# One pool of seven PSUM banks, and ScalarE's measured pace in the planner of a fused attention and MLP kernel

## The chip, the cores and the metric

The kernel runs on one core of a Trainium2 chip. The metric is the time of one execution on the device in microseconds (us); the span in a profile runs from the first to the last instruction and is about 1.8 us shorter. PE is TensorE, ACT is ScalarE, DVE is VectorE, POOL is GpSimd, SP is SyncE.

## The reference

```python
def reference(A_x, A_wq, A_wk, A_wv, A_wo, B_x, B_w1, B_w2):
    # x: 2048 x 512 bf16; 32 query heads of 16, one key head and one value head
    xn = layernorm(x)
    q = (xn @ wq) split into 32 heads; k = xn @ wk; v = xn @ wv
    s = softmax(q k^T / 4) v, heads joined, @ wo
    h = silu(xn @ w1)             # 512 -> 1792
    g = silu(h @ w2)              # 1792 -> 512
    return x + s * g
```

Scores are 32 heads x 2048 queries x 2048 keys. The exponentials of this many numbers are the bulk of the work outside TensorE. (The code of the reference, which is longer, is put here in short form.)

## The kernel before

The program is not written down instruction by instruction. A planner simulates the five engines with assumed durations and latencies, picks the next instruction for each engine, and emits what it picked; on the chip, semaphores enforce the dependencies, and each engine keeps the planned order.

A score tile is 128 keys x 512 queries of one head, f32, one PSUM bank. There are 2048 of them. A tile goes one of two ways. ScalarE takes two or three banks in one `Exp` instruction and writes bf16, which then needs one value product on PE. Or VectorE converts the tile to an integer whose bits are an approximate exponential; GpSimd (or VectorE) makes three shifted copies, and the tile then needs four value products.

```python
A_BANKS = ((0, 1, 2), (3, 4, 5))      # two halves for ScalarE
OB = 6                                # accumulates the value products of a group
POOL_BANKS = (7,)                     # everything else: projections, VectorE's tiles
...
LAT = {                               # ns from an instruction's end to its being seen
    (PE, AC): 221.0, (PE, DV): 221.0, (PE, PE): 0.0,
    (AC, PE): 402.0, (AC, DV): 390.0, (AC, AC): 250.0, ...
...
def s_phase_ready():                  # may PE start the next score phase?
    ub = st["fill"] % 2
    banks = A_BANKS[ub]
    if len(units) >= 2 and units[-2].exp is None:
        return None
    if lent.get(ub) is not None and lent[ub].op is None:
        return None
    ...
    for b in banks:                   # all three banks of the half
        r = max(r, pl.ready(PE, (), [("ps", b)]))
...
op = pl.place(AC, 0.8333 * NQ * n + T_AF, lambda a: a.activation(
    pa_sb[:, s * NQ:(s + n) * NQ], ps[:, b0 * 512:(b0 + n) * 512], ACT.Exp), ...)
```

Score matmuls use four row tiles of 32 and fill up to four banks at once. Value products, projections and the MLP use four column tiles of 32; I call four such matmuls a round. In the listings below, L756 (before) and L776 (after) are the score matmuls, L1056 and L1079 the value products, L458 and L466 the projections and the MLP, L1297 and L1341 the exponentials, L937 and L962 VectorE's score conversions.

The softmax here doesn't subtract the row's maximum and nothing guards it: scores larger than these inputs give would overflow.

## Time and profile before

| | before |
|---|---|
| time, median | 716.7 us |
| span of the profiled run | 715.0 us |
| ScalarE busy | 676.6 us, 95% |
| tiles on ScalarE / on VectorE | 1392 / 656 |
| exp instructions (3, 2, 1 banks) | 93, 556, 1 |

One warning ahead: the mean length of a record is not an engine's pace, since ScalarE's records overlap.

### The profile page before, as it was taken

The numbers are of one execution on the slowest core, as the hardware profiler recorded it, in microseconds if no ns is written. First come the engines' busy times: TensorE is split into PE (matmuls) and PEld (weight loads), VectorE is DVE, ScalarE is ACT, GpSimd is POOL, SyncE is SP. The second block draws the span as 40 slices with busy tenths as digits, with TensorE's granted clock in tenths as the row PEclk, the third lists the DMA queues.
The fourth block names the chain that finished last, engine by engine and source line by source line (L and its number), as shares of the span: only waits on it lengthen the run. The fifth ranks groups of instructions, "written<-read, shape, count | busy, mean of one in ns | idle before, by whom it ended". The sixth has DMA issues, their size and how long they took to land.

```text
span 715.0 us, 20429 instructions
## 1 busy us (share of the span) xinstructions
PE 669.9 (94%) x8693; PEld 191.2 (27%) x8693; DVE 604.8 (85%) x1039; ACT 676.6 (95%) x729; POOL 484.6 (68%) x472
## 2 busy tenths in 40 slices
PE   5799999999999999999999999998999999999996
PEld 3332222222222222222222222222232222222233
DVE  8778889989889898888887898899888898899865
ACT  3699999999999999999999999999989999999992
POOL 2037777877866777867777768778626677878780
PEclk9899999999999999999999999999999999999999
DMA  9300000000000000000000000000000000000000
GB/s 314 101 17 1 2 2 2 2 1 3 2 2 2 23 25 17 2 1 2 2 2 2 1 3 24 24 17 1 2 2 2 2 1 17 17 17 17 2 2 31
DMA packets 11434, 12.61 MB, mean 18 GB/s; under 512 B 1809, under 2 KB 10769, under 8 KB 11345
## 3 DMA queue, kind: packets, MB, share of 16 engines
q1 hardware_dynamic: 10288, 11.28, 4.9%
q8 instruction: 70, 1.15, 0.7%
q10 hardware_dynamic: 1056, 0.03, 0.1%
q14 instruction: 20, 0.16, 0.1%
HBM read 8.95 MB, written 2.10 MB: 15 GB/s over the span
## 4 chain that ended last, share of the span: by engine, by line
ACT 79%; PE 12%; DVE 7%; issue 1%; DVEq 0%
ACT pa_sb L1297 75%; PE ps L1056 4%; ACT t_sb L584 4%; PE ps L458 4%; PE ps L756 3%; DVE db_sb L937 2%; DVE ds_sb L991 1%; DVE stats_sb L405 1%; ACT t_sb L607 1%; PE ps L474 1%; DVE f_sb L1073 0%; DVE otr_sb L1077 0%; DVE xn_sb L434 0%; PE ps L500 0%; DVE fin_sb L621 0%
## 5 line engine op out<-in xcount | busy, mean ns | idle before, releaser
L1297 ACT ACTIVATE pa_sb<-ps 128x1024 bf16<-128x1024 f32 (+1 forms) x650 | 660.8, 1282 | 13.7 <-PE ps L756 12.0
L996 POOL INT64_ADD ds_sb<-db_sb x461 | 480.7, 1059 | 212.4 <-PE ps L1056 143.9
L937 DVE TENSOR_SCALAR db_sb<-ps 128x512 uint16<-128x512 f32 x656 | 436.4, 685 | 68.7 <-PE ps L756 62.3
L756 PE MATMUL ps<-qt_sb,kt_sb 32*128 32x512 bf16 x2048 | 256.1, 385 | 21.7 <-ACT pa_sb L1297 10.4
L1056 PE MATMUL ps<-ds_sb,v_sb 128*32 128x512 bf16 x1968 | 228.1, 383 | 0.9 <-DVE ds_sb L991 0.5
L1056 PE MATMUL ps<-pa_sb,v_sb 128*32 128x512 bf16 x1392 | 215.6, 384 | 0.3 <-ACT pa_sb L1297 0.3
L1056 PE MATMUL ps<-db_sb,v_sb 128*32 128x512 bf16 x656 | 154.4, 384 | 6.4 <-DVE f_sb L1073 6.3
L756 PEld LDWEIGHTS ps<-qt_sb,kt_sb 32*128 32x128 bf16 x2048 | 65.8, 91 | 305.9 <-ACT pa_sb L1297 245.7
L1056 PEld LDWEIGHTS ps<-ds_sb,v_sb 128*32 128x32 bf16 x1968 | 56.8, 95 | 55.7 <-issue 36.9
L458 PE MATMUL ps<-xnT_sb,w_sb 128*32 128x512 bf16 x896 | 69.2, 384 | 0.3 <-DVE db_sb L937 0.3
L458 PE MATMUL ps<-w_sb,u_sb 128*32 128x512 bf16 x896 | 68.5, 384 | 0.9 <-DVE db_sb L937 0.9
L1056 PEld LDWEIGHTS ps<-pa_sb,v_sb 128*32 128x32 bf16 x1392 | 54.8, 95 | 36.5 <-issue 23.3
L1056 PEld LDWEIGHTS ps<-db_sb,v_sb 128*32 128x32 bf16 x656 | 38.2, 95 | 29.8 <-DVE f_sb L1073 12.8
L584 ACT ACTIVATE t_sb<-ps 128x512 bf16<-128x512 f32 x56 | 46.0, 822 | 0.0
L586 DVE SCALAR_TENSOR_TENSOR u_sb<-t_sb,ps 128x512 bf16<-128x512 bf16 x56 | 38.1, 681 | 9.1 <-ACT t_sb L584 8.2
L991 DVE TENSOR_SCALAR ds_sb<-db_sb 128x2048 uint16<-128x2048 uint16 x31 | 26.5, 871 | 1.8 <-PE ps L1056 1.6
L458 PEld LDWEIGHTS ps<-w_sb,u_sb 128*32 128x32 bf16 x896 | 17.0, 94 | 29.3 <-issue 22.4
L1073 DVE STREAM_TRANSPOSE f_sb<-ps 128x512 f32<-128x512 f32 x32 | 22.7, 708 | 1.5 <-PE ps L1056 1.2
L458 PEld LDWEIGHTS ps<-xnT_sb,w_sb 128*32 128x32 bf16 x896 | 14.8, 94 | 27.5 <-issue 21.5
L609 DVE SCALAR_TENSOR_TENSOR tmp_sb<-t_sb,ps 128x512 bf16<-128x512 bf16 x16 | 11.0, 685 | 11.4 <-ACT t_sb L607 11.3
L458 PE MATMUL ps<-xnT_sb,wq_sb 128*32 128x512 bf16 x256 | 20.0, 399 | 0.0
L1077 DVE TENSOR_TENSOR otr_sb<-f_sb,rcp_sb 128x256 bf16<-128x256 f32 x32 | 18.7, 588 | 0.2
(54 smaller groups left out, 168.9 us busy)
## 6 DMA issues: line engine op xcount, KB each, us to landing
w_sb<-in_B_w_dram SPq DMA_DIRECT2D x2, 1792.0 KB, 13.0
xr_sb<-in_A_x_dram SPq DMA_DIRECT2D x16, 128.0 KB, 2.6
out_dram<-ob_sb SPq DMA_DIRECT2D x16, 128.0 KB, 1.7
ds_sb<-in_A_x_dram SPq DMA_DIRECT2D x3, 512.0 KB, 6.8
ds_sb<-in_A_x_dram SPq DMA_DIRECT2D x4, 128.0 KB, 2.9
wq_sb<-in_A_wq_dram SPq DMA_DIRECT2D x1, 512.0 KB, 4.8
wo_sb<-in_A_wo_dram SPq DMA_DIRECT2D x1, 512.0 KB, 15.3
kt_sb<-kt_sb SPq DMA_DIRECT2D x4, 64.0 KB, 3.4
```

The lines of the kernel that those rows point to most:

```text
L458: last = h.matmul(bank(b)[32 * j:32 * (j + 1), 0:n], lhsT=lhs(j), rhs=rhs, start=start, stop=stop, tile_position=(0, 32 * j), skip_group_c ...
L584: t1 = Task(AC, 477.0, lambda a: a.activation(t_sb[:, k, :], bank(b), ACT.Tanh, scale=0.5), [("ps", b)], [("t", k)], 0)
L586: t2 = Task(DV, T_P, lambda v: v.scalar_tensor_tensor(out=u_sb[:, ft, :], in0=t_sb[:, k, :], scalar=1.0, in1=bank(b), op0=ALU.add, op1=ALU ...
L609: t2 = Task(DV, T_P, lambda v: v.scalar_tensor_tensor(out=tmp_sb[:, tt % 8, :], in0=t_sb[:, k, :], scalar=1.0, in1=bank(b), op0=ALU.add, o ...
L756: return pe.matmul(bank(b), lhsT=kt_sb[32 * i:32 * i + 32, g % 2, kt * P:(kt + 1) * P], rhs=qt_sb[32 * i:32 * i + 32, (g // 2) % NQR, :], ...
L937: bt.P[i] = pl.add(Task(DV, T_P, lambda v, b=b, i=i, bb=bt.b: v.tensor_scalar(db_sb[:, bb, i * NQ:(i + 1) * NQ], bank(b), 128.0 * LOG2E, 1 ...
L991: whole[DV] = pl.add(Task(DV, T_SH, lambda v: v.tensor_scalar(ds_sb[:, s, :], db_sb[:, bt.b, :], SHIFT[j - 1], 1.0, op0=ALU.add, op1=ALU.m ...
L996: whole[PO] = pl.add(Task(PO, T_P64, lambda g: g.int64_add(ds_sb[:, s, :].bitcast(U64), db_sb[:, bt.b, :].bitcast(U64), words), reads, ds_ ...
L1056: h = pe.matmul(bank(OB)[32 * i:32 * (i + 1), :], lhsT=lhs, rhs=rhs, start=s0, stop=s1, tile_position=(0, 32 * i), skip_group_check=True)
L1073: t1 = pl.add(Task(DV, T_TR, lambda v: v.transpose(f_sb[:, k, :], bank(OB)), [("ps", OB)], [("F", k)], 1, [norm.get(("m", g - 2))]))
L1077: t3 = pl.add(Task(DV, 332.0, lambda v: v.tensor_tensor(o3[:, :, val:val + DH], f3[:, :, val:val + DH], rcp_sb[:, k, :].unsqueeze(2).to_br ...
L1297: op = pl.place(AC, 0.8333 * NQ * n + T_AF, lambda a: a.activation(pa_sb[:, s * NQ:(s + n) * NQ], ps[:, b0 * 512:(b0 + n) * 512], ACT.Exp) ...
```

## The change

The intent: PE should fill any free banks, so that ScalarE never waits for a particular half; ScalarE takes one bank, or two neighbours; projections take any bank. The planner gets ScalarE's measured pace. Near the end of a head group it lets projection and MLP rounds start ahead of schedule and gives the group's value products priority. The core of the diff:

```diff
-T_P, T_SH, T_TR, T_AF = 600.0, 600.0, 630.0, 51.0
-T_P64, DV_MIN, T_LIB = 1060.0, 4, 6500.0
+T_P, T_SH, T_TR, T_AF = 600.0, 600.0, 630.0, 64.3
+T_P64, DV_MIN, T_LIB = 1035.0, 4, 300.0
+NEAR, AHEAD = 24, 0.6
+WIDE, NMIN, EARLY = 2, 2, 200.0
-    (AC, PE): 402.0, (AC, DV): 390.0, (AC, AC): 250.0, (AC, PO): 410.0, (AC, SP): 410.0,
+    (AC, PE): 157.0, (AC, DV): 140.0, (AC, AC): 110.0, (AC, PO): 160.0, (AC, SP): 160.0,
-    A_BANKS = ((0, 1, 2), (3, 4, 5))
-    POOL_BANKS = (7,)
+    BANKS = (0, 1, 2, 3, 4, 5, 7)
 ... s_phase_ready:
-            for b in banks:
-                r = max(r, pl.ready(PE, (), [("ps", b)]))
+            bt = bank_times()                     # free banks, earliest first
+            n = min(n, 4)
+            while n > NMIN and bt[n - 1][0] > need:
+                n -= 1
 ... do_S: how many of the phase's tiles VectorE gets
+            if n <= 1:
+                want = 1 if ab > 2 * A_LOW else 0
+            elif n == 2:
+                want = 1 if ab > A_LOW else 0
+            else:
+                want = 2 if n == 4 or ab > A_LOW else 1
+            want = min(want, 2 if bl < TWO_LIMIT else 1 if bl < ONE_LIMIT else 0)
 ... near the end of a group
+        def closing():
+            ...
+            return nleft[g] == 0 and sum(tot[g, i] - done[g, i] for i in range(4)) <= NEAR
-                if jb.pace > progress() + 1e-9:
+                near = n >= NPRO and closing()
+                if jb.pace > progress() + (AHEAD if near else 1e-9):
-            if pr and pr[0] == "go" and (a_pressure() >= PRESS):
+            if pr and pr[0] == "go" and (a_pressure() >= PRESS or closing()):
 ... act_step: each tile is a unit of its own; neighbours are taken together
-                    pa_sb[:, s * NQ:(s + n) * NQ], ps[:, b0 * 512:(b0 + n) * 512], ACT.Exp),
+                    pa_sb[:, s * NQ:(s + n) * NQ].rearrange("p (b n) -> p b n", n=NQ), ps3[:, b0:b1 + 1:step, :], ACT.Exp),
```

Cut here: the bookkeeping; smaller numbers (tanh and copies planned at 490 ns in place of 477, `TWO_LIMIT` 1300 in place of 1500, `ONE_LIMIT` 2500 new); how the planner estimates ScalarE's need and VectorE's backlog; that VectorE's score conversions all get the highest priority; the first case of `closing`, while the group before is not yet normalised; that the run-ahead also passes over the limit on waiting tiles; and an optional early copy out of PSUM that is switched off.

## The prediction

> **What bounds the kernel now.** I read the page first, then the table by stretches, the chain of waits, the groups by form, and last the timeline of the final 18 us.
>
> ```profile
> PE 669.9 (94%) x8693; PEld 191.2 (27%) x8693; DVE 604.8 (85%) x1039; ACT 676.6 (95%) x729; POOL 484.6 (68%) x472
> ...
> ACT 79%; PE 12%; DVE 7%; issue 1%; DVEq 0%
> ```
>
> ScalarE (ACT) carries 79% of the chain that ended last, so its work is what the time is made of. PE looks as busy, but a matmul's record overlaps the next one's, so its 94% needs a count of its own (below). The stretches say where ScalarE is not full:
>
> ```profile
> 15.00:50.00 35.00, 28.94 (x376) 12.09 (x377) 25.08 (x75) 28.24 (x25) 3.40 (x4) 0.90 0.30 91
> 50.00:150.00 100.00, 96.56 (x1248) 25.95 (x1236) 86.97 (x140) 100.00 (x113) 78.14 (x77) 1.00 0.01 2
> 150.00:250.00 100.00, 95.95 (x1239) 26.00 (x1236) 87.92 (x142) 98.30 (x108) 71.16 (x67) 1.00 0.02 6
> ...
> 450.00:550.00 100.00, 94.95 (x1248) 26.46 (x1248) 87.01 (x140) 95.69 (x104) 66.33 (x63) 1.00 0.02 7
> 550.00:650.00 100.00, 95.74 (x1222) 25.43 (x1214) 88.81 (x145) 99.83 (x113) 74.00 (x73) 1.00 0.03 10
> ```
>
> After the length, the columns are PE, PEld, DVE, ACT and POOL, in us. In 15 to 50 us ScalarE loses 6.8 us (the prologue feeds it late). From 50 to 700 us it loses only about 7, of which 4.3 lie between 450 and 550 and 1.7 between 150 and 250. So idle time holds little to be won; the work itself must shrink, or the ends must.
>
> The true pace of ScalarE stands in the chain, where an unbroken run of one form is one row:
>
> ```profile
> 50.48 6.42 ACT pa_sb L1297 x7
> 56.90 0.49 ACT t_sb L584
> 57.38 3.67 ACT pa_sb L1297 x4
> ```
>
> 6.42/7 and 3.67/4 are 0.917 us for two banks, and 0.49 for one. The difference is 0.427 for a bank, so each instruction costs about 0.064 beside its data, and three banks take 1.344. The groups give the counts, but their means (1229 ns for two banks) are not the pace, since records overlap:
>
> ```profile
> L1297 ACT ACTIVATE pa_sb<-ps 128x1024 bf16<-128x1024 f32 x556 | 548.2, 1229 | 4.9 <-PE ps L756 4.7
> ...
> L1297 ACT ACTIVATE pa_sb<-ps 128x1536 bf16<-128x1536 f32 x93 | 141.8, 1602 | 8.9 <-PE ps L756 7.3 <-PE ps L1056 1.3
> ```
>
> 556 x 0.9176 + 93 x 1.344 + one single and 70 tanh before the end at 0.49 = 510.2 + 125.0 + 34.8 = 670.0 us. The first exp starts at 15.1 and the last ends at 700.3: 685.2 us, so 15.2 idle, close to the 13.8 that the stretches show. The last part is the tail:
>
> ```profile
> 695.86 4.42 ACT L1297 ACTIVATE pa_sb<-ps 128x1536 bf16<-128x1536 f32 x3
> ...
> 698.40 3.19 PE L458 MATMUL ps<-w_sb,u_sb 128*32 128x512 bf16 x56
> ...
> 703.36 3.19 PE L458 MATMUL ps<-w_sb,u_sb 128*32 128x512 bf16 x56
> 706.38 2.98 PE L458 MATMUL ps<-wo_sb,on_sb 128*32 128x512 bf16 x52
> ```
>
> After the last exp the program takes 14.7 us, and PE spends two blocks of 3.2 us there on the second MLP product (z), one ahead of the last attention rounds and one ahead of the output projection.
>
> **What the Trainium skill says.** "ScalarE: Activation LUTs", What ACT_TABLE_LOAD costs: 0.833 ns per element, 186 ns fixed with immediate operands, and back-to-back instructions overlap by about 93. The trace agrees on the slope (0.427 us for 512) and shows 64 ns where that leaves 93. "Perfetto Trace Analysis", DVE / Act Engine Instruction: a record runs from leaving the execution FIFO to the write acknowledgement, after which the semaphore still has to propagate. That is how records of 1229 ns fit a pace of 917. "TensorEngine Tiling (Array Packing)", Key Properties: a change of tiling mode drains TensorE. The trace agrees: in the chain at 524 to 527 us a round of four column tiles next to its like costs 0.21 to 0.22, a score phase 0.32, and the round after it 0.33; so each visit to the score mode costs two switches of about 0.11. "PSUM — Partial Sum Buffer", The four PSUM rules: a matmul's output stays within one bank; the score matmuls here write 512 f32 each, so a phase can take any free banks.
>
> **The change, part by part.** The built programs give counts, no times.
>
> 1. *Work moved off ScalarE.* Score tiles are 2048 in both. ScalarE took 556 x 2 + 93 x 3 + 1 = 1392, and takes 600 x 2 + 148 = 1348. VectorE takes 700 in place of 656. ScalarE's new work: 600 x 0.9176 + 148 x 0.491 + 72 x 0.49 = 550.6 + 72.7 + 35.3 = 658.6 us, against 670.0 + 1.0 for the two tail tanh. 44 tiles fewer save 18.8; 98 more instructions at 0.064 give back 6.3. On the path: -11.4 between first and last exp.
> 2. *The tail.* In the new order no z block stands behind the last score phase; only the output projection's 16 rounds do. Estimate from rows of the old tail: last rounds and semaphores 0.55 after the last exp, transpose to transpose 2.2 (702.94 to 705.15), a first projection closed 0.6 later, the four final steps 3.8 (708.77 to 712.59), the store 2.4: 9.6 in place of 14.7, so -5. The five single exps at the end, fed by phases of three and one tile, give back an estimated 1.
> 3. *The planner's model of ScalarE.* It planned 904 ns for two banks with 402 until others see the end; now 917.6 and 157. The sum from start to visible is 1.31 before, 1.07 now. Starts in an unbroken run are 903 apart early, while the ends are 917 apart, so the old pair was late early in a run and about right far into it. This makes banks count as free some 0.2 us sooner; in stretches where ScalarE already works 100% it gives nothing.
> 4. *One pool of banks.* A phase no longer waits for a whole half of three, and a bank lent to VectorE no longer blocks its half. It also lets jobs run ahead near the end of a group, where the idle of 182 and 527 us lies. I leave the prologue's 6.8 as it is and main idle at 7: the elastic banks should remove some, point 5 adds some.
> 5. *PE pays.* A tile on VectorE needs four value products in place of one: 3 x 44 = 132 more matmuls. By runs in the built order PE goes from 1631 rounds and 636 visits to the score mode to 1678 and 649. At 0.216 a round and 0.43 a visit: 352 + 273 = 626 us before, 362 + 279 = 642 now, of about 683 and 673 us there. PE goes from 91% to 95% of its window. VectorE: 44 x 0.62 (four of its score conversions took 2.48 in the chain) + 5 more shifts x 0.87 = +32, to about 636 us, 91% of a shorter span. POOL: 28 x 1.04 = +29, to about 514.
>
> Sum: first exp 15.1 + work 658.6 + idle 6.8 + 7 + end 1 + tail 9.6 = 698.1 us of span. A run is 1.7 above its span (716.7 against 715.0), so 699.8; I put 699.5.
>
> **The rivals.**
> - *PE becomes the bound.* For: 95% with every round unavoidable, while the page's waits still show PE held at each group's end by the transpose of the output bank (12.8 us in front of loads). Against: the pool is there so that PE need not stop for one particular bank, and 246 us of "PEld ps L756 <- ACT pa_sb" are waits for banks, which are the slack. If it wins, ScalarE idles 10 to 15 us more in mid-kernel: 705 to 712.
> - *VectorE holds the banks.* Every score tile for VectorE occupies a shared bank until converted, now at high priority; with 91% busy, a transpose or reciprocal chain delays the release and ScalarE gets single banks or none. For: 148 single exps, a sign that two neighbours were often not ready. Against: long runs of pairs stand in most of the order. It would cost 3 to 8 us: 703 to 708.
> - *Idle vanishes as well.* If the pool removes most of the 7 us in mid-kernel and part of the prologue's: 690 to 694.
>
> **Range and chances.** The first two steps are counts and measured paces, worth 15.4 us together, just over 2% (14.3). What decides is whether idle time grows by more than about 1 or not. The two costly rivals lie above the 2% line (702.3), the kind one below. I take 691 to 708, and 0.66 for faster by over 2%, 0.32 for within, 0.02 for slower.
>
> **What would show each step.** ScalarE's groups: 600 at 128x1024 and 148 at 128x512, runs of pairs again 0.917 apart, singles 0.49. Its busy time should be near 662 to 668, its idle between 50 us and the last exp near 7. The tail after the last exp should be about 10 us with no rows of w_sb,u_sb. The score phases' loads should wait for ScalarE far less than 246 us. Wrong would be: ScalarE idle of over 15 us behind PE score phases in mid-kernel (PE the bound); many waits of score loads for db_sb (VectorE the bound); singles further apart than 0.49.

## The result

The changed kernel takes 695.0 us (694.98 to 695.54, 4 runs), the kernel before 716.2 in the same rounds (715.5 to 717.1). The ratio is 0.9705, 95% interval 0.9688 to 0.9722. Ratios here are the mean time of one kernel's runs over the mean of the other's of the same rounds, so not quite the ratio of the medians.

The head of the page after the change, and its chain of waits:

```profile
PE 670.8 (97%) x8843; PEld 193.8 (28%) x8843; DVE 627.9 (91%) x1088; ACT 667.4 (96%) x827; POOL 519.5 (75%) x500
...
PE 62%; ACT 24%; DVE 12%; issue 1%; ACTq 0%; DVEq 0%
```

ScalarE's busy time fell by 9 us and PE's stayed, in 22 us less. The chain went from 79% ScalarE to 62% PE. The table by stretches (length, then PE, PEld, DVE, ACT, POOL):

```profile
15.00:50.00 35.00, 31.54 (x469) 12.87 (x469) 30.15 (x78) 31.73 (x43) 9.21 (x9) 1.00 0.31 96
50.00:150.00 100.00, 98.84 (x1289) 27.59 (x1289) 89.83 (x147) 99.99 (x117) 79.70 (x78) 1.00 0.01 2
150.00:250.00 100.00, 97.99 (x1312) 27.69 (x1304) 92.38 (x150) 98.59 (x122) 80.62 (x76) 1.00 0.03 10
...
450.00:550.00 100.00, 97.20 (x1279) 26.97 (x1271) 92.11 (x150) 98.83 (x144) 82.11 (x79) 1.00 0.01 2
550.00:650.00 100.00, 99.51 (x1315) 27.45 (x1316) 92.74 (x151) 99.60 (x118) 81.08 (x78) 1.00 0.04 12
```

From 15 to 50 us ScalarE now loses 3.3 us, not 6.8. VectorE went from 85 to 89% of a stretch to 90 to 93%. ScalarE's groups by form, and the end of the timeline:

```profile
L1341 ACT ACTIVATE pa_sb<-ps 128x1024 bf16<-128x1024 f32 x600 | 574.1, 1063 | 6.5 <-PE ps L776 5.7
L1341 ACT ACTIVATE pa_sb<-ps 128x512 bf16<-128x512 f32 x148 | 83.4, 642 | 0.9 <-PE ps L776 0.6
```
```profile
682.65 1.14 ACT L1341 ACTIVATE pa_sb<-ps 128x512 bf16<-128x512 f32 x2
...
683.85 3.74 PE L466 MATMUL ps<-wo_sb,on_sb 128*32 128x512 bf16 x56
684.28 0.72 DVE L1096 STREAM_TRANSPOSE f_sb<-ps 128x512 f32<-128x512 f32 x1 [6.18 <-PE ps L1079]
...
690.07 0.75 DVE L643 TENSOR_TENSOR ob_sb<-fin_sb,xr_sb 128x512 bf16<-128x512 bf16 x2
```

Behind the last exp (it ends at 683.8) there are only its value product and the output projection, no rows of the second MLP product. The mean record of two banks fell from 1229 to 1063 ns, while the pace did not change: in the trace after, the ends of pairs in a row stand 917 ns apart (median), and a single ends 490 ns after its forerunner. Records stretch along an unbroken run, and the runs are shorter now; whether that is the whole of the fall was not worked out.

Where the 21.8 us of span went can be counted. I walk ScalarE's instructions with the measured paces (0.9176 us for two banks, 1.344 for three, 0.491 for one, 0.49 for tanh). Time in which no work of this kind is pending, between the first exp's start and the last exp's end, is idle. So the column of work is a count times a pace, and idle is what the trace adds. The tail is what follows the last exp's end.

| us | first exp at | ScalarE work | idle to 50 us | idle after 50 us | tail | span |
|---|---|---|---|---|---|---|
| before | 15.1 | 670.1 | 7.3 | 7.8 | 14.7 | 715.0 |
| predicted for after | 15.1 | 658.6 | 6.8 | 7 + 1 | 9.6 | 698.1 |
| after | 13.1 | 658.6 | 3.6 | 8.5 | 9.4 | 693.2 |
| difference measured | -2.0 | -11.5 | -3.7 | +0.7 | -5.3 | -21.8 |

### The profile page after: what moved, and what is told of

It reads as the page before. It is cut to its first block, busy times and chain, and to the rows that moved or that the text cites. A ratio compares the mean times of both kernels' runs of the same rounds, so it can differ in the third digit from the quotient of the medians.

```text
span 693.2 us, 20821 instructions
## 1 busy us (share of the span) xinstructions
PE 670.8 (97%) x8843; PEld 193.8 (28%) x8843; DVE 627.9 (91%) x1088; ACT 667.4 (96%) x827; POOL 519.5 (75%) x500
## 4 chain that ended last, share of the span: by engine, by line
PE 62%; ACT 24%; DVE 12%; issue 1%; ACTq 0%; DVEq 0%
PE ps L1079 25%; ACT pa_sb L1341 23%; PE ps L776 21%; PE ps L466 15%; DVE db_sb L962 5%; DVE ds_sb L1014 2%; ACT t_sb L588 1%; DVE stats_sb L413 1%; DVE f_sb L1096 1%; DVE ob_sb L643 1%; DVE u_sb L590 0%; DVE otr_sb L1100 0%; DVE xn_sb L442 0%; DVE fin_sb L640 0%; DVE xnT_sb L493 0%
## 5 line engine op out<-in xcount | busy, mean ns | idle before, releaser
L1341 ACT ACTIVATE pa_sb<-ps 128x1024 bf16<-128x1024 f32 (+1 forms) x748 | 639.7, 980 | 7.4 <-PE ps L776 6.3
L1019 POOL INT64_ADD ds_sb<-db_sb x489 | 515.5, 1072 | 158.9 <-DVE db_sb L962 102.9
L962 DVE TENSOR_SCALAR db_sb<-ps 128x512 uint16<-128x512 f32 x700 | 449.9, 682 | 44.1 <-PE ps L776 40.0
L1079 PE MATMUL ps<-ds_sb,v_sb 128*32 128x512 bf16 x2100 | 265.1, 383 | 0.2
L1079 PE MATMUL ps<-pa_sb,v_sb 128*32 128x512 bf16 x1348 | 242.8, 383 | 1.8 <-DVE ds_sb L1014 1.0
L1079 PE MATMUL ps<-db_sb,v_sb 128*32 128x512 bf16 x700 | 171.0, 383 | 2.8 <-DVE f_sb L1096 2.8
L776 PEld LDWEIGHTS ps<-qt_sb,kt_sb 32*128 32x128 bf16 x2048 | 63.9, 91 | 281.6 <-ACT pa_sb L1341 145.8
L1079 PEld LDWEIGHTS ps<-ds_sb,v_sb 128*32 128x32 bf16 x2100 | 65.9, 95 | 60.7 <-issue 40.0
L1079 PEld LDWEIGHTS ps<-pa_sb,v_sb 128*32 128x32 bf16 x1348 | 61.2, 95 | 45.1 <-issue 23.6
L1014 DVE TENSOR_SCALAR ds_sb<-db_sb 128x2048 uint16<-128x2048 uint16 x36 | 37.3, 1039 | 0.1
L466 PE MATMUL ps<-wo_sb,on_sb 128*32 128x512 bf16 x256 | 20.4, 383 | 0.1
## 6 DMA issues: line engine op xcount, KB each, us to landing
w_sb<-in_B_w_dram SPq DMA_DIRECT2D x2, 1792.0 KB, 13.1
```

Of the source, the lines that this page charges most:

```text
L466: last = h.matmul(bank(b)[32 * j:32 * (j + 1), 0:n], lhsT=lhs(j), rhs=rhs, start=start, stop=stop, tile_position=(0, 32 * j), skip_group_c ...
L776: return pe.matmul(bank(b), lhsT=kt_sb[32 * i:32 * i + 32, g % 2, kt * P:(kt + 1) * P], rhs=qt_sb[32 * i:32 * i + 32, (g // 2) % NQR, :], ...
L962: bt.P[i] = pl.add(Task(DV, T_P, lambda v, b=b, i=i, bb=bt.b: v.tensor_scalar(db_sb[:, bb, i * NQ:(i + 1) * NQ], bank(b), 128.0 * LOG2E, 1 ...
L1014: whole[DV] = pl.add(Task(DV, T_SH, lambda v: v.tensor_scalar(ds_sb[:, s, :], db_sb[:, bt.b, :], SHIFT[j - 1], 1.0, op0=ALU.add, op1=ALU.m ...
L1019: whole[PO] = pl.add(Task(PO, T_P64, lambda g: g.int64_add(ds_sb[:, s, :].bitcast(U64), db_sb[:, bt.b, :].bitcast(U64), words), reads, ds_ ...
L1079: h = pe.matmul(bank(OB)[32 * i:32 * (i + 1), :], lhsT=lhs, rhs=rhs, start=s0, stop=s1, tile_position=(0, 32 * i), skip_group_check=True)
```

## The experiments

Each experiment ran beside the kernel before (715.7 to 715.8 us in these rounds). Where I say "against after", I compare two ratios to the kernel before and multiply by 716; the intervals are about 0.2% wide on each side, so at 2 us such a difference is at the noise. Walks are of one profiled run each. The wrong results meant on purpose still passed the comparison with the reference.

The theory after reading the result: ScalarE's work and its idle make the time as predicted, and the prologue gain comes from PE's warm-up matmuls. The rivals: PE is the bound now (the chain says so), or VectorE's late release of banks is what leaves ScalarE idle (104 us of score loads now wait for it, against 30 before):

```profile
PEld ps L756 <- ACT pa_sb L1297: 245.7, 531, 1.2
...
PEld ps L756 <- DVE db_sb L937: 30.2, 60, 0.7
```
```profile
PEld ps L776 <- ACT pa_sb L1341: 145.8, 348, 0.8
PEld ps L776 <- DVE db_sb L962: 104.1, 227, 1.2
```

The views are the waits, first of before, then of after: who waited for whom, us in total, times, the longest.

### Parts of the change

**b_lib: one planner number in the kernel before.**

```diff
-T_P64, DV_MIN, T_LIB = 1060.0, 4, 6500.0
+T_P64, DV_MIN, T_LIB = 1060.0, 4, 300.0
```

> The kernel before with one planner number changed (the first GpSimd library call planned at 300 ns in place of 6500): every count on ScalarE and VectorE stays, only the warm-up matmuls go from 2 to 16. Theory: PE ran its first projections at half pace because nothing kept it running before 8.2 us; with the warm-up the first exp starts 2 us earlier and the idle of 15 to 50 us shrinks by some 2 to 3, so the run takes 4 to 5 us less: about 711.5. Rival: the start is hidden by what follows (VectorE's layer norm sets the prologue), and the run stays within 1 us of 716.

714.6 us, ratio 0.9982 (0.9967 to 0.9997): 1.3 us less, not 4 to 5. The mechanism is there, the size is not. The timeline of PE's start, before and then with the number changed:

```profile
1.52 1.03 PE L1272 MATMUL ps<-zer_sb 128*128 128x512 bf16 x2 [1.52 <-DVE zer_sb L374]
...
11.96 1.92 PE L458 MATMUL ps<-xnT_sb,wq_sb 128*32 128x512 bf16 x16
```
```profile
1.52 5.28 PE L1272 MATMUL ps<-zer_sb 128*128 128x512 bf16 x16 [1.52 <-DVE zer_sb L374]
...
10.91 1.04 PE L458 MATMUL ps<-xnT_sb,wq_sb 128*32 128x512 bf16 x16
```

The same 16 projection matmuls take 1.92 us where PE had been idle and 1.04 after the warm-up. The Trainium skill says in "TensorE: Matmul & The Clock Gate", Part 1, that the default state is throttled, and activity releases it. The durations agree; the profile's granted clock, 1.00 from 0 to 15 us in the kernel before, does not show it. With the old number the planner's PE clock jumps to GpSimd's assumed end of 6.5 us while it finds nothing to do, and 14 of the 16 warm-up matmuls are never placed: the plan's first PE instruction stood at 7.2 us, with the new number at 1.4 (from the built plans; no trace shows a plan). But the first exp moved by only 1.3 us, from 15.1 to 13.8, and the idle that follows it stayed at 6.7 (7.3). In both, the granted clock is 0.77 between 20 and 35 us. In the changed kernel it is 1.00 there, and ScalarE loses 3.3 us of this stretch in place of 6.0 in the kernel before. The lines are of before, of the changed kernel, of b_pe_more and of a_pe_less (two runs from further down):

```profile
20.00:35.00 15.00, 11.09 (x114) 4.73 (x114) 10.68 (x37) 8.98 (x7) 0.00 (x0) 0.77 0.22 70
```
```profile
20.00:35.00 15.00, 13.01 (x204) 6.28 (x196) 11.94 (x38) 11.73 (x19) 0.00 (x0) 1.00 0.26 82
```
```profile
20.00:35.00 15.00, 10.55 (x146) 4.80 (x144) 11.44 (x38) 10.38 (x9) 0.00 (x0) 1.00 0.23 74
```
```profile
20.00:35.00 15.00, 13.65 (x193) 6.38 (x185) 11.12 (x36) 10.43 (x17) 0.00 (x0) 0.89 0.24 75
```

So the number accounts for 1.3 us of the prologue's 5.7 by the times (1.9 by the walk). The rest can be split in part. The edits of b_pe_more and a_pe_less touch nothing before 37 us, so up to there b_pe_more has the order of the kernel before, and a_pe_less that of the changed one. With the old order ScalarE loses 6.0 us at a clock of 0.77 and 4.6 at 1.00; with the new one 4.6 at 0.89 and 3.3 at 1.00. So the clock differs from run to run of one order. Of the 2.7 us between the profiles of before and after in this stretch, 1.4 goes with the clock of the profiled runs and 1.3 with the order. What sets the clock was not tested.

**b_all_but_pool: everything but the pool, in the kernel before** (the planner's numbers and the `closing` lines of the diff above).

> The kernel before with every part of the change except the pool of banks: library number, ScalarE pace and latencies, and the run-ahead near a group's end. Counts from the build: ScalarE work 671.4 us (as before), PE 646 score visits and 1662 rounds (637 us against 625), no z block in the tail. Theory that ScalarE's work decides: before less the start (4 to 5) and the tail (5) = 706 to 708. Rival, that the pool's own flexibility is not the source and pace plus run-ahead are: 700 or less.

705.8 us, ratio 0.9860 (0.9841 to 0.9879), as the first theory had it. Its walk: first exp 13.4, work 671.5, idle 4.6 and 3.6, tail 9.5, span 702.7. So the start, the tail and even less idle than in the changed kernel are to be had with two halves of three banks. What it does not have is the smaller ScalarE work: 671.5 against 658.6, and 12.9 is more than the 9.5 between the two spans. Its VectorE takes 656 tiles, as before, and a_oldpace below, which has the pool with the old numbers, 644. So the move of 44 tiles took the pool and the numbers together. The rule that shares a phase's tiles out (`do_S`) was changed along with the pool, and which of the two it needs was not separated.

**a_no_closing: the changed kernel without the run-ahead.**

```diff
         def closing():
+            return False
```

> The changed kernel without the run-ahead near a group's end (the test always says no). From the build: 672 tiles on VectorE, 585 pairs and 206 singles, ScalarE work 673.2 us (after: 658.5), PE work 641.4 us (after: 641.3), no z in the tail. If ScalarE's work sets the end: 695 + 14.7 = about 709. If PE's work sets it: 695 to 699, since PE has the same rounds.

734.2 us, ratio 1.0251 (1.0234 to 1.0268): slower than the kernel before, and outside both expectations. The walk gives 673.3 us of work, as expected, but 31.6 us of idle after 50 us, against 8.5. One such place, in the timeline:

```profile
161.32 0.83 PE L466 MATMUL ps<-zer_sb 128*32 128x256 bf16 x24
162.40 0.70 DVE L1096 STREAM_TRANSPOSE f_sb<-ps 128x512 f32<-128x512 f32 x1
...
163.16 0.82 PE L1079 MATMUL ps<-db_sb,v_sb 128*32 128x512 bf16 x9 [1.01 <-DVE f_sb L1096]
...
164.04 1.51 ACT L1342 ACTIVATE pa_sb<-ps 128x512 bf16<-128x512 f32 x2 [2.76 <-PE ps L1079]
```

At the end of a group PE has only filler (`zer_sb`) to do. The transpose that frees the output bank starts late on VectorE, the value products wait for it, and ScalarE waits 2.76 us for value products, which still read its output buffers. In all, ScalarE waits 14.7 us for value products and 11.0 for score phases after 50 us. What keeps the transpose (`f_sb`) here is VectorE's own work, two shifts, as the chain of waits shows:

```profile
159.78 2.70 DVE ds_sb L1014 x2
162.48 0.64 DVE f_sb L1096
```

VectorE makes 55 shifts in this run in place of 36. With the run-ahead the plan puts projections and MLP rounds into such moments, and the last products of the group first. How much of the idle comes from that, and how much from the shifts and from the smaller share of tiles that the new order brought along, was not separated.

**a_oldpace: the changed kernel with the planner's old ScalarE numbers.**

```diff
-T_P, T_SH, T_TR, T_AF = 600.0, 600.0, 630.0, 64.3
+T_P, T_SH, T_TR, T_AF = 600.0, 600.0, 630.0, 51.0
-    (AC, PE): 157.0, (AC, DV): 140.0, (AC, AC): 110.0, (AC, PO): 160.0, (AC, SP): 160.0,
+    (AC, PE): 402.0, (AC, DV): 390.0, (AC, AC): 250.0, (AC, PO): 410.0, (AC, SP): 410.0,
 ... 490 back to 477 for tanh and copies, 1035 back to 1060 for GpSimd's shift
```

> The changed kernel with the old ScalarE numbers in the planner (51 ns and 402 ns latencies, tanh 477, GpSimd shift 1060). From the build: 644 tiles on VectorE, 622 pairs and 160 singles, ScalarE work 684.6 us, PE 674 visits and 1633 rounds = 642.5 us. If ScalarE's work sets the end: 695 + 26 = about 721, slower than the kernel before. If PE's work does: 696.

720.6 us, ratio 1.0066 (1.0045 to 1.0088): as expected from ScalarE's work alone. The walk: first exp 13.6, work 684.6, idle 3.2 and 7.0, tail 9.4. The idle hardly changed; the split did, 644 tiles on VectorE in place of 700. In the prediction I had called this model worth nothing where ScalarE is always busy. In the planner it is worth the whole split: with banks seen as free 0.2 us later, PE's phases got fewer free banks (134 phases of four banks in the trace, 192 in after's), and the rule that gives VectorE up to two tiles of a phase of four fired less often. The run changed the pace, the latencies and the GpSimd number at once; which of them decides was not tested.

These four runs are not a sum of parts. The thresholds were tuned for all parts together, and the planner answers any change with another order; each run tells what its own order costs.

### What bounds the changed kernel

The next six leave the order as it is: the planner is told nothing, only what an instruction does is changed.

**a_pe_more and b_pe_more: more PE work.** The first round of each h tile is issued twice; the second starts the sum afresh, so the result stays right.

```diff
-                    return lambda pe: col4(pe, b, lambda j: w1_sb[...], xnT_sb[...], dc == 0, dc == NDC - 1)
+                    def emit(pe):
+                        for _ in range(2 if dc == 0 else 1):
+                            h = col4(pe, b, lambda j: w1_sb[...], xnT_sb[...], dc == 0, dc == NDC - 1)
+                        return h
+                    return emit
```

> The changed kernel, order and plan untouched, with the first round of each of the 56 h tiles issued twice (same result): 56 x 0.216 = 12.1 us more PE work. Theory that PE is the bound now: +10 to +12, about 706. Theory that ScalarE still is: the extra rounds fall into PE's slack, +0 to +4.

704.4 us, ratio 0.9827 (0.9809 to 0.9845): 8.7 us more than after, of 12.1 added. The walk puts nearly all of it in idle after 50 us, 17.3 against 8.5.

> The same 56 extra rounds in the kernel before, where PE had more slack (626 of 683 us): both theories expect less than in the changed kernel, +2 to +5 us, 718 to 721.

717.2 us, ratio 1.0006 (0.9985 to 1.0027): no difference from the kernel before. In the walk, idle after 50 us is 9.9 against 7.8, and idle before 50 us 5.1 against 7.3, which goes with the clock of the prologue above: the edit first acts at 46 us. So before, PE took most of these rounds into its slack, at a cost of about 2 us, and now it has little room left.

**a_pe_less: less PE work.**

```diff
+                    n = NQ if dc < 2 else 64
-                                           xnT_sb[:, dc, c * NQ:(c + 1) * NQ], dc == 0, dc == NDC - 1)
+                                           xnT_sb[:, dc, c * NQ:c * NQ + n], dc == 0, dc == NDC - 1, n)
```

> The changed kernel with the third and fourth round of every h tile cut to 64 of 512 columns (wrong result on purpose): 112 x 0.187 = 20.9 us less PE work, order untouched. PE the bound: the run falls until ScalarE has no idle left, by 7 to 9 us, to 686 to 688. ScalarE the bound: -0 to -3.

693.2 us, ratio 0.9674 (0.9653 to 0.9695): 2.2 us less than after, the answer of "ScalarE the bound". Idle after 50 us went from 8.5 to 6.5 and no further, so most of what idle is left does not go away with this cut. (The profiled run was the slowest of its four, 694.5 against 692.7 to 693.5, and lost 1.4 us more before 50 us, at the clock shown above.)

**a_act_less: less ScalarE work.**

```diff
-                    pa_sb[:, s * NQ:(s + n) * NQ].rearrange(...), ps3[:, b0:b1 + 1:step, :], ACT.Exp),
+                    pa_sb[:, s * NQ:(s + n) * NQ].rearrange(...)[:, :, 0:NQ - 32],
+                    ps3[:, b0:b1 + 1:step, 0:NQ - 32], ACT.Exp),
```

The columns left out are set to zero once, by GpSimd at the start.

> The changed kernel with every exp over 480 of the 512 columns of each bank (wrong result on purpose): 1348 x 0.0267 = 36 us less ScalarE work, order untouched. PE the bound: little, -2 to -6 us. ScalarE the bound: -20 us or more, until PE's 642 us and its waits stop it, about 675.

693.2 us, ratio 0.9669 (0.9648 to 0.9690): 2.6 us less than after, the answer of "PE the bound". ScalarE's work fell to 622.6 us and its idle after 50 us rose to 41. Some of the cut was lost at the start: with the extra GpSimd instruction the first exp starts 0.6 us later. Each cut alone speaks for the other engine.

**a_both_less: both cuts at once.**

> The changed kernel with both cuts at once (wrong result on purpose): 20.9 us less PE work and 36 us less ScalarE work, order untouched. Each cut alone took 1.9 us. Theory that PE and ScalarE are jointly the bound, each right behind the other: 10 to 17 us less, 678 to 685. Rival, that a third thing (VectorE's release of banks, 104 us of score loads wait for it) holds both: 2 to 4 us less, 691 to 693.

684.8 us, ratio 0.9565 (0.9551 to 0.9580): 10 us less than after, at the near edge of what the joint bound gives, and about twice the sum of the two cuts (2.2 and 2.6 by the ratios; the 1.9 of the expectation is by medians). In this order PE and ScalarE bind together, each right behind the other. But 20.9 us and 36 us were taken and only 10 came, so something else holds too. VectorE is the candidate; a cut there together with one of these was not run.

**a_dve_less: less VectorE work.**

```diff
-                    db_sb[:, bb, i * NQ:(i + 1) * NQ], bank(b), 128.0 * LOG2E, ...
+                    db_sb[:, bb, i * NQ:(i + 1) * NQ - 64], bank(b)[:, 0:NQ - 64], 128.0 * LOG2E, ...
```

Here too GpSimd sets the columns left out to zero once, at the start.

> The changed kernel with VectorE's 700 score conversions over 448 of 512 columns (wrong result on purpose): 700 x 0.067 = 47 us less VectorE work, order untouched. VectorE the bound or the holder of banks: 6 us less or more, 689 or below. PE and ScalarE the bound together: 0 to 3 us less.

689.8 us, ratio 0.9636 (0.9620 to 0.9652): 4.9 us less than after, between the two expectations, and the largest answer of any single cut. It came although the first exp started 1.4 us later in this run. The walk: work 658.6, unchanged, and idle after 50 us 2.6 in place of 8.5. So most of the mid-kernel idle goes away when VectorE gets faster. But this was also the largest cut: for each us that was meant to be taken, PE's cut and this one both gave 0.10 us, and ScalarE's 0.07. VectorE's busy time fell by 35 us, not 47, and score loads still wait 93.0 us for it, against 104.1. So VectorE holds the time along with the other two, and is not shown to be the first of the three. A place where one sees its part in the changed kernel is the chain at the end of a group:

```profile
108.86 0.35 PE ps L776 x3
109.21 0.02 issue
109.24 0.69 DVE db_sb L962
109.93 0.63 DVE f_sb L1096
110.56 0.04 issue
110.60 0.61 PE ps L1079 x8
```

PE's score phase is followed by a conversion, which keeps the transpose waiting on VectorE, and the transpose keeps the next value products waiting on PE.

### Versions with other thresholds

**a_tuned.**

```diff
-T_P64, DV_MIN, T_LIB = 1035.0, 4, 300.0
+T_P64, DV_MIN, T_LIB = 1035.0, 6, 300.0
-MARGIN, MARGIN_END = 16, 28
+MARGIN, MARGIN_END = 16, 20
-HOLD, Q_LEAD = 1000.0, 3.3
+HOLD, Q_LEAD = 600.0, 3.3
-START_Z, START_H = 8, 14
+START_Z, START_H = 12, 14
-WIDE, NMIN, EARLY = 2, 2, 200.0
+WIDE, NMIN, EARLY = 2, 2, 250.0
-A_LOW, JOB_SPARE = 1000.0, 0
+A_LOW, JOB_SPARE = 900.0, 0
```

> The changed kernel with six of the planner's thresholds moved (start of z at 12 tiles waiting, hold 600, early 250, low mark 900, end margin 20, VectorE shifts from 6 waiting). From the build: ScalarE work 652.0 us (6.5 less), PE 642.2 us (0.9 more), 712 tiles on VectorE. If both bind together, PE gives no room: within 2 us of 695. If ScalarE's work alone counts: about 689.

687.3 us (687.2 to 687.6), ratio 0.9602 (0.9587 to 0.9616), with a correct result: 28 us under the kernel before and 7.4 under the changed one. It beats both. The walk: first exp 13.5, work 652.1, idle 3.7 and 5.9, tail 10.5. The 6.5 us of ScalarE work came through in full and idle fell too, although PE's count of work did not shrink. VectorE converts 12 tiles more but makes fewer shifts itself (31 in place of 36; it takes one only when six wait, and GpSimd's share rises), so its busy time is the same: 626.2 us against 627.9. That this is why PE gave way was not tested: six thresholds moved at once.

**a_tuned2.**

```diff
-T_P64, DV_MIN, T_LIB = 1035.0, 4, 300.0
+T_P64, DV_MIN, T_LIB = 1035.0, 5, 300.0
-MARGIN, MARGIN_END = 16, 28
+MARGIN, MARGIN_END = 12, 16
-START_Z, START_H = 8, 14
+START_Z, START_H = 8, 12
-WIDE, NMIN, EARLY = 2, 2, 200.0
+WIDE, NMIN, EARLY = 2, 3, 200.0
-A_LOW, JOB_SPARE = 1000.0, 0
+A_LOW, JOB_SPARE = 1000.0, 1
```

> The changed kernel with other thresholds moved (phases of at least three banks unless late, a bank spared for a due job, h jobs from 12 tiles waiting, margins 12 and 16, VectorE shifts from 5 waiting). From the build: ScalarE work 644.5 us (14.0 less), PE 635 visits and 1686 rounds = 637.2 us (4.1 less), 728 tiles on VectorE (17 us more work there). Joint bound: about 691, limited by PE. VectorE's extra work holding banks: 695 or more.

694.9 us, ratio 0.9704 (0.9689 to 0.9718): the same as after, the number of the VectorE theory. ScalarE's work fell by 14.0 us and PE's by 4.1, and none of it came through: idle after 50 us went from 8.5 to 17.0, idle before 50 from 3.6 to 6.8, the tail from 9.4 to 11.8. VectorE's busy time is 640.8 us, 13 more than after. That fits the theory, but the order changed as well, so the cause is not shown.

## Why the prediction was right

It said 699.5 (691 to 708) and faster by over 2%; 695.0 came.

- *Work moved off ScalarE.* Right. The 658.6 us is the same count times the same paces, so it agrees by itself; what the trace adds is that the paces held (917 and 490 ns between ends), that the groups are 600 and 148, and that ScalarE's busy time, 667.4, lies in the 662 to 668 that was given. b_all_but_pool and a_oldpace, whose times follow from their ScalarE work (671.5 and 684.6), bear the step out.
- *The tail.* Right: 9.4 against 9.6. It is owed neither to the run-ahead nor to the pool as such: a_no_closing, without the one, has 9.4, and b_all_but_pool, without the other, 9.5. It depends on where the order puts the last MLP tiles.
- *The prologue is the term that was mis-sized.* "I leave the prologue's 6.8 as it is", with the first exp at 15.1, measured 3.6 and 13.1: 5.2 us (6.8 - 3.6 and 15.1 - 13.1), which more than covers the 4.9 between the predicted and the measured span. The built orders showed the sign, 16 warm-up matmuls in place of 2, and the prediction passed over it. b_lib shows 1.3 us of it as the warm-up's, and 1.4 goes with the clock that the profiled runs happened to have.
- *Mid-kernel idle.* 7 and 1 for the end were put, 8.5 came. That points 4 and 5 would about cancel was a guess, and luck has a part in it: small edits move this idle far, to 31.6 without the run-ahead, 17.3 with 12.1 us more PE work, 17.0 in a_tuned2 and 2.6 with VectorE relieved.
- *"In stretches where ScalarE already works 100% it gives nothing"*, said of the planner's ScalarE numbers, was wrong: a_oldpace is 3.7% slower than after (1.0066 over 0.9705), because the numbers decide the split. The predicted time did not suffer from this, since the split was counted from the built order.
- *Rival: PE becomes the bound.* Half right. The chain went to PE, and added PE work now costs 8.7 of 12.1 us where it cost nothing before. But the 10 to 15 us of extra idle did not come, and taking PE work away gave 2.2.
- *Rival: VectorE holds the banks.* Its mechanism is there: 104 us of waits for it, and 4.9 us from making its conversions shorter. Its cost was inside the 8.5 us of idle and not on top, so the time stayed below 703.
- *"The score phases' loads should wait for ScalarE far less than 246 us"* came true for ScalarE (145.8), but the wait went to VectorE: 145.8 + 104.1 = 249.9, against 245.7 + 30.2 = 275.9. Waits of a load are no measure of slack here.
- VectorE's busy time rose by 23 us and not 32: 44 more conversions added 13.5 us of busy time (436.4 to 449.9), not 27. Busy time counts overlapping records once.
- *"A run is 1.7 above its span"* sets the median 716.7 against the span of another run; the run with the span of 715.0 took 716.85, so it is 1.8. This is too small to matter.

## What to carry to other kernels

Count the pace of an engine from an unbroken run in the chain and not from the mean length of records; then a count of the built instructions times that pace, plus start, idle and tail, gives a time that can be checked term by term. When a chain moves from one engine to another, this does not say that the new one is the bound: take work away from each engine alone and from two at once, with the order kept, before choosing what to shorten. In a kernel that a planner orders, compare the start and the end of the built orders as carefully as the middle, and test a part only with the knowledge that thresholds were tuned for all parts together.

## What the Trainium skill lacked or had wrong

- "ScalarE: Activation LUTs" gives 186 ns fixed and 93 ns of overlap, so 93 ns for each instruction in a row, and does not say in which memory the operands lay. "Perfetto Trace Analysis", Optimizing Scalar/DVE Operations, has about 93 ns for ScalarE on SBUF and 51 on PSUM. In these runs, from PSUM to SBUF, it is 64, between the two (7 two-bank instructions in 6.42 us, 0.49 us for one bank). The slope of 0.833 ns agrees.
- "Perfetto Trace Analysis" explains what a ScalarE record spans, but not that records grow along an unbroken run: starts of two-bank instructions stand 903 to 904 ns apart while ends stand 917 apart, and one record lasts from 1018 to 1364 ns for the same work.
- "TensorEngine Tiling (Array Packing)" says that a change of mode drains TensorE and gives no time; here the change costs about 0.11 us each way (0.32 us for a score phase and 0.33 for the round after it, against 0.21 to 0.22).
- "TensorE: Matmul & The Clock Gate" has the cold start, and warns that the clock events in a trace were seen to be unreliable; it has no case of a cold start that they miss. Here is one: the kernel before shows a granted clock of 1.00 from 0 to 15 us, while 16 projection matmuls took 1.92 us there and 1.04 after a warm-up.
- No page treats engines that share PSUM banks and bind together: cuts of 20.9 us on PE and 36 us on ScalarE gave 2.2 and 2.6 us alone and 10 together.
